# Attention and two MoE layers on one core: earlier first queries, a filled first hole, nine products for the shared tile

## The chip, the cores and the metric

One core of one Trainium2 chip runs the whole program in one launch. The metric is the device time of that launch in microseconds (us). Of the kernel before, three runs took 697.0, 698.44 and 698.81 us; the median is 698.44 us. One further run was profiled.

## The reference

Three stages follow one another. Attention has 2 batches of 8 heads, 1152 keys and 576 queries (two neighbouring queries are averaged first) of 64 dimensions. Then a softplus layer with 2048 and a gated layer with 1536 hidden columns follow, on 1152 tokens of 512. All arrays are fp32.

```python
q_pool = q.reshape(B, H, S // factor, factor, D).mean(axis=3)
scores = scale * np.matmul(q_pool, k.transpose(0, 1, 3, 2))
scores = scores - np.max(scores, axis=-1, keepdims=True)
attn = np.exp(scores)
attn = attn / (np.sum(attn, axis=-1, keepdims=True) + 1e-09)
attn_out = np.matmul(attn, v)
...
h = x @ w_in
g = np.maximum(h, 0.0) + np.log1p(np.exp(-np.abs(h)))
x = g @ w_out
...
xn = x / rms * rms_g
out = (silu(xn @ w_gate) * (xn @ w_val)) @ w_out
```

## The kernel before

**Split operands.** Every fp32 operand of a product is split into a rounded part (h) and the small remainder (l), both stored as fp32r. A head has 64 dimensions, half of the array's 128 rows. So a head's key tile `kk` holds the rounded keys (K high) in one half of the partitions and the remainders (K low) in the other, and the queries stand in both halves. One product of `qh` with `kk` then gives high by high plus high by low; a second one with `ql` gives the rest. A tile of 128 queries against 1152 keys is done in three thirds of 384 keys: six products.

**Tiles of a pair.** Heads are taken in pairs (A and B), eight pairs. 576 queries are four tiles of 128 and one rest of 64. The rests of both heads share one tile: A's 64 queries stand in columns 0 to 63, B's in 64 to 127, and zeros fill the other half of each operand. `qk` (L437) issues twelve products for this shared tile: qh and ql of A, qh and ql of B, three thirds each.

**A tile's way.** TensorE writes the scores into PSUM (one buffer per head letter); VectorE takes the maximum over 1152 columns (L466); ScalarE takes the exponential (L468); TensorE transposes it in groups of four 128x128 blocks into one of two PSUM banks `t` (L487, the shared tile's L774); ScalarE or VectorE copies each bank to SBUF (L258, L260); TensorE multiplies by V (L508).

**The start.** `prep(0)` (L346) loads the first pair. Its keys `kr` come in thirds on SyncE's queue; the first 128 queries of each head (`qr` for A, `p` for B, two pieces each) on ScalarE's queue, behind `rgs` and behind an activation table load; the other queries follow on SyncE's queue. Each query sum, rounding, remainder and each K low third is an instruction of its own. Meanwhile TensorE does 16 transposes of the identity that nobody reads (`heat`, L791).

**The order.** Nothing is ordered by hand. `Plan` collects all operations with their engines, estimated durations and dependences, and `run` (L147) simulates a list schedule, which fixes each engine's instruction order; several copies may go to either of two engines. TensorE keeps the order in which the program was written. `WAIT` (L175) says when a more urgent operation may pass another. `EARLY` (L36) is the number of weight pieces unpacked during attention into slots that exist from the beginning; `MIDDLE` more follow when half of attention's buffers are closed.

Of the kernel before, what the change touches and what calls it, by code (L numbers as in the profile page):

```python
# [12 lines left out]
F32 = mybir.dt.float32  # L13
# [22 lines left out]
EARLY = 10  # L36
# [4 lines left out]
WAIT = 2.0  # L41
WARM = 16
# [168 lines left out]
def body(ctx: ExitStack, tc: tile.TileContext, kT, qT, v, w1, w1o, wg, wv, w2o, rg, outT):  # L211
    nc = tc.nc
    ctx.enter_context(tc.manual_schedule())
    nc.scalar.preload_act_table_set("exp_and_others")
# [12 lines left out]
    nc.scalar.dma_start(out=rgs, in_=rg)  # L227
# [71 lines left out]
    def decode(n):  # L299
# [26 lines left out]
        if b in third:  # L326
# [5 lines left out]
    qx = [[[fixed("ea"[z], f"q{s}{'AB'[h]}{z}", [P, NF * P + P], F32R) for s in "hl"] for h in range(2)]  # L332
          for z in range(2)]
# [4 lines left out]
    for z in range(2):  # L338
        for h in range(2):
            for s in range(2):  # L340
                c = NF * P + (D if h == 0 else 0)
                op([dve(D)], lambda e, b=qx[z][h][s], c=c: copy(e, b()[:, c:c + D], zero), w=[(qx[z][h][s], "z")])
# [3 lines left out]
    def prep(pb):  # L346
# [9 lines left out]
        qcuts = ((0, slice(0, P), P), (1, slice(P, SQ), SQ - P))  # L356

        def load_q(h, c, cut, m, queue):
            for z in range(2):
                load(lambda z=z: qr[h]()[z * D:z * D + D, :, cut], qT[n + h][:, :, cut], m // 2, [(qr[h], (z, c))], queue)  # L360

        for h in range(2):
            qr.append(ring("a", "p1", [P, 2, SQ], F32, 2) if first and h else ring("e", "qr", [P, 2, SQ]))
            qs.append(ring("a", "y", [P, SQ]) if first and h else ring("e", "qs", [P, SQ]))
            if first:
                load_q(h, *qcuts[0], "ACTQ")
        pairs = kT[n:n + 2].rearrange("a d s -> (a d) s")
        if first:
            for c, cut, m in kcuts:
                load(lambda cut=cut: kr()[:, cut], pairs[:, cut], 192, [(kr, c)])  # L370
        else:
            load(kr, pairs, 576, [(kr, None)])
        for h in range(2):
            if first:
                load_q(h, *qcuts[1], "SP")
            else:
                for z in range(2):
                    load(lambda h=h, z=z: qr[h]()[z * D:z * D + D], qT[n + h], 288, [(qr[h], (z, 0)), (qr[h], (z, 1))])
# [13 lines left out]
        def sum_q(h, cut, m, c):  # L392
            op([dve(m), pool(m)], lambda e: tt(e, qs[h]()[:, cut], qr[h]()[:, 0, cut], qr[h]()[:, 1, cut], ALU.add),
               r=[(qr[h], (z, x)) for z in range(2) for x in c], w=[(qs[h], c)])

        for h in range(2):
# [3 lines left out]
            if first:  # L400
                c, cut, m = qcuts[0]
# [526 lines left out]
```

## Time and profile before

| | |
|---|---|
| median of three runs | 698.44 us |
| profiled execution | 697.78 us |
| its span, first to last instruction | 695.6 us |
| TensorE matmul busy | 681.2 us, 98% |
| VectorE busy | 430.7 us, 62% |
| ScalarE busy | 335.2 us, 48% |
| GpSimd busy | 111.9 us, 16% |

Attention takes about the first 267 us, the softplus layer and the gated layer the rest. Engines are PE (TensorE), PEld (its weight loads), DVE (VectorE), ACT (ScalarE), POOL (GpSimd), SP (SyncE); an engine with a q at its end is the queue's issue of DMAs. A row of the timeline gives start, length and the idle time before with what ended it. Products are pipelined, so the length of a single row (337 ns) is longer than their distance; the chain of waits shows the distance.

### The profile page before, as it was taken

Reading aid. Unit: us, or ns where it says so; the run is one execution under the profiler, and the core shown is the slowest. Engines: PE = TensorE matmul, PEld = TensorE weight load, DVE = VectorE, ACT = ScalarE, POOL = GpSimd, SP = SyncE. Lnnn points to the kernel's source line nnn. Section 1 sums busy time; section 2 is a strip of 40 time slices with the busy share of each in tenths; the row PEclk is TensorE's granted clock in tenths of the full one; section 3 lists DMA queues with packets and bytes.
Section 4 is the critical chain, followed back from the end, with each engine's and each line's share of the span. In section 5 each row is a group of like instructions: output and inputs, shape, how many; then the busy total and the mean of one; then the engine's idle time right before and its main releaser. Section 6 shows DMA issues by size and latency. Waiting matters only on the chain.

```text
span 695.6 us, 12413 instructions
## 1 busy us (share of the span) xinstructions
PE 681.2 (98%) x5071; PEld 657.5 (95%) x5071; DVE 430.7 (62%) x741; ACT 335.2 (48%) x617; POOL 111.9 (16%) x115
## 2 busy tenths in 40 slices
PE   6999999999999999999999999999999999999997
PEld 5989899898889889999999999999999999999997
DVE  6778778877877778987425267887875332222222
ACT  4877878887788784654212243464452210010001
POOL 1531426425341132000000000011121000000000
PEclk9999999999999999999999999999999999999999
DMA  7355424262412213554000023343441100010001
GB/s 209 124 152 140 130 83 135 55 181 96 120 38 76 79 62 111 182 176 141 28 1 1 3 89 122 127 147 119 163 146 56 46 0 1 1 46 0 1 1 45
DMA packets 21221, 59.77 MB, mean 86 GB/s; under 512 B 3823, under 2 KB 6830, under 8 KB 21166
## 3 DMA queue, kind: packets, MB, share of 16 engines
q1 hardware_dynamic: 20446, 58.73, 26.8%
q8 instruction: 39, 0.64, 0.4%
q10 hardware_dynamic: 720, 0.26, 0.2%
q14 instruction: 16, 0.13, 0.1%
HBM read 56.59 MB, written 2.39 MB: 85 GB/s over the span
## 4 chain that ended last, share of the span: by engine, by line
PE 70%; ACT 0%; DVE 0%; issue 0%
PE s L618 15%; PE s L620 15%; PE s L619 15%; PE t L620 5%; PE t L618 5%; PE t L619 5%; PE t L508 3%; PE s L450 3%; PE t L487 2%; PE t L774 0%; PE s L688 0%; ACT pt L258 0%; PE s L716 0%; PE t L566 0%; DVE raw L260 0%
## 5 line engine op out<-in xcount | busy, mean ns | idle before, releaser
L618 PE MATMUL s<-x,w 128*128 128x384 f32 x348 | 117.4, 337 | 0.5 <-ACT rs L258 0.5
L466 DVE TENSOR_REDUCE nm<-s 128x1 f32<-128x1152 f32 x72 | 97.7, 1357 | 31.7 <-PE s L450 28.1
L620 PE MATMUL s<-x,w 128*128 128x384 f32 x348 | 116.7, 335 | 0.0
L619 PE MATMUL s<-x,w 128*128 128x384 f32 x348 | 116.6, 335 | 0.0
L468 ACT ACTIVATE p<-s,nm 128x1152 f32<-128x1152 f32 x72 | 88.2, 1225 | 12.9 <-DVE nm L466 11.1
L258 ACT COPY pt<-t 128x512 f32<-128x512 f32 (+1 forms) x146 | 76.0, 528 | 36.4 <-PE t L487 29.8
L487 PE MATMUL t<-ident,p 128*128 128x128 f32 x576 | 85.7, 281 | 3.6 <-ACT pt L258 2.2
L740 ACT ACTIVATE g<-s 128x384 f32<-128x384 f32 x36 | 17.7, 492 | 139.7 <-PE s L620 139.7
L487 PEld LDWEIGHTS t<-ident,p 128*128 128x128 f32 x576 | 66.6, 142 | 16.3 <-issue 5.1
L618 PE MATMUL s<-gh,w 128*128 128x384 f32 x243 | 81.5, 335 | 0.0
L620 PE MATMUL s<-gh,w 128*128 128x384 f32 x243 | 81.5, 335 | 0.0
L619 PE MATMUL s<-gl,w 128*128 128x384 f32 x243 | 81.4, 335 | 0.0
L508 PE MATMUL t<-pt,v 128*64 128x128 f32 (+1 forms) x1440 | 80.1, 265 | 0.0
L508 PEld LDWEIGHTS t<-pt,v 128*64 128x64 f32 x1440 | 71.3, 137 | 7.3 <-issue 6.3
L618 PEld LDWEIGHTS s<-x,w 128*128 128x128 f32 x348 | 65.4, 188 | 1.0 <-ACT rs L258 0.8
L619 PEld LDWEIGHTS s<-x,w 128*128 128x128 f32 x348 | 65.4, 188 | 0.0
L620 PEld LDWEIGHTS s<-x,w 128*128 128x128 f32 x348 | 65.4, 188 | 0.0
L263 DVE TENSOR_TENSOR gl<-g,gh 128x384 fp32r<-128x384 f32 x84 | 48.7, 580 | 11.5 <-ACT gh L258 9.3
L312 ACT ACTIVATE t<-raw 128x512 f32<-128x512 f32 x68 | 44.6, 672 | 15.9 <-DVE w L263 10.4
L260 DVE CAST gh<-g 128x384 fp32r<-128x384 f32 x61 | 22.1, 362 | 45.3 <-PE t L620 39.3
L640 ACT ACTIVATE g<-s 128x384 f32<-128x384 f32 x36 | 17.7, 492 | 64.4 <-PE s L620 62.9
L322 DVE SCALAR_TENSOR_TENSOR t<-t,t 128x512 int32<-128x512 int32 x68 | 47.2, 694 | 1.5
(141 smaller groups left out, 1195.3 us busy)
## 6 DMA issues: line engine op xcount, KB each, us to landing
raw<-in_w_dram SPq DMA_DIRECT2D x16, 512.0 KB, 4.2
raw<-in_w1o_dram SPq DMA_DIRECT2D x16, 512.0 KB, 3.4
qr<-in_qT_dram SPq DMA_DIRECT2D x28, 288.0 KB, 4.3
raw<-in_wg_dram SPq DMA_DIRECT2D x12, 512.0 KB, 3.5
raw<-in_wv_dram SPq DMA_DIRECT2D x12, 512.0 KB, 3.6
raw<-in_w2o_dram SPq DMA_DIRECT2D x12, 512.0 KB, 3.5
v<-in_v_dram SPq DMA_DIRECT2D x16, 288.0 KB, 3.2
kr<-in_kT_dram SPq DMA_DIRECT2D x7, 576.0 KB, 5.5
```

The costliest lines, as they stand in the source:

```text
L258: nc.scalar.copy(out, in_)
L260: engines[e].tensor_copy(out, in_)
L263: engines[e].tensor_tensor(out=out, in0=in0, in1=in1, op=o)
L312: o = op([("ACT", 0.68)], lambda e: nc.scalar.activation(out=t0(), in_=word(1).bitcast(F32), scale=2.0 ** -112, **(dict(func=AF.Prelu, alp ...
L322: op([dve(DM)], lambda e: nc.vector.scalar_tensor_tensor(out=t0().bitcast(I32), in0=t0().bitcast(I32), scalar=3, in1=t1(), op0=ALU.logical ...
L466: u["mx"] = op([dve(S, psum=True)], lambda e: nc.vector.tensor_reduce(out=nm(), in_=sc()[:, :, :N], axis=AX.XY, op=ALU.max, negate=True), ...
L468: o = op([("ACT", 1.42)], lambda e: nc.scalar.activation(out=pr(), in_=sc()[:, :, :N], func=AF.Exp, bias=nm(), accum_out=s["den"]()[:, col ...
L487: nc.tensor.transpose(t()[:, i * P:(i + 1) * P], pr[:, c * P:(c + 1) * P], ident)
L508: nc.tensor.matmul(t()[h * D:h * D + D, :n], lhsT=s["v"][h]()[:, c, :], rhs=rhs, start=(c == 0), stop=(c == CK - 1))
L618: nc.tensor.matmul(out, lhsT=w[:, 0, cols], rhs=hi, start=start, stop=False)
L619: nc.tensor.matmul(out, lhsT=w[:, 0, cols], rhs=lo, start=False, stop=False)
L620: nc.tensor.matmul(out, lhsT=w[:, 1, cols], rhs=hi, start=False, stop=stop)
```

## The change

- The first 128 queries of head A are the first transfer on both queues, one piece on each; the first key third follows on ScalarE's queue, the other two on SyncE's, then B's first queries. The array of queries is laid out so that the two neighbours of the first 128 lie side by side: a piece is one run of 256 numbers per partition. The table load moves behind ScalarE's two DMAs, `rgs` to the end of attention.
- The first maximum waits, as a dependence, for the K low thirds and the first query remainders of both heads; the copy `kh` below waits for that maximum.
- 20 instead of 16 idle transposes at the start, and 16 more (`WAKE`) between the products of the first two tiles and the first transposes of exponentials.
- The shared tile gets nine products: qh of A and qh of B with their `kk`, and one with `qm` and `kh` for both heads. `qm` holds A's 64 remainders in its upper left and B's in its lower right quarter, zeros elsewhere; `kh` is the rounded keys of both heads, one under the other, a new copy of 128x1152 per pair. Remainder by remainder is dropped for this tile.
- Query sums are cut at 128, 224 and 224 columns instead of twice 288; the first pair's are only done on VectorE.
- `EARLY` is 9 instead of 10, `WAIT` 3.5 instead of 2.0, and the first ten loads of each queue keep their written order.

```diff
-EARLY = 10
+EARLY = 9
...
-WAIT = 2.0
-WARM = 16
+WAIT = 3.5
+WARM = 20
+WAKE = 16
...
-    nc.scalar.preload_act_table_set("exp_and_others")
...
-    nc.scalar.dma_start(out=rgs, in_=rg)
...
-    def load(out, src, kb, w, queue="SP"):
+    issued = {"SP": [], "ACTQ": []}
+
+    def load(out, src, kb, w, queue="SP", lat=2.2):
         q = nc.sync if queue == "SP" else nc.scalar
-        return op([(queue, 0.6 + max(0, kb / 220 - 0.6))], lambda e: q.dma_start(out=out(), in_=src), w=w, lat=2.2)
+        o = op([(queue, 0.6 + max(0, kb / 220 - 0.6))], lambda e: q.dma_start(out=out(), in_=src), w=w, lat=lat,
+               after=issued[queue][-1:] if len(issued[queue]) < 10 else ())
+        issued[queue].append(o)
+        return o
...
-    qx = [[[fixed("ea"[z], f"q{s}{'AB'[h]}{z}", [P, NF * P + P], F32R) for s in "hl"] for h in range(2)]
-          for z in range(2)]
+    qx = [[[fixed("ea"[z], f"q{s}{'AB'[h]}{z}", [P, NF * P + (P if s == "h" else 0)], F32R) for s in "hl"]
+           for h in range(2)] for z in range(2)]
+    qm = [fixed("ea"[z], f"qm{z}", [P, P], F32R) for z in range(2)]
...
-        qcuts = ((0, slice(0, P), P), (1, slice(P, SQ), SQ - P))
-
-        def load_q(h, c, cut, m, queue):
+
+        def load_q(h, c, queues=("SP", "SP")):
+            cut = slice(0, 2 * P) if c == 0 else slice(2 * P, 2 * SQ) if c == 1 else slice(0, 2 * SQ)
             for z in range(2):
-                load(lambda z=z: qr[h]()[z * D:z * D + D, :, cut], qT[n + h][:, :, cut], m // 2, [(qr[h], (z, c))], queue)
+                parts = [(qr[h], (x, z)) for x in range(2) if c in (x, None)]
+                load(lambda z=z: qr[h]()[z * D:z * D + D, cut], qT[n + h][:, cut], (cut.stop - cut.start) // 4, parts, queues[z])
...
-            if first:
-                load_q(h, *qcuts[0], "ACTQ")
+        if first:
+            load_q(0, 0, ("SP", "ACTQ"))
         pairs = kT[n:n + 2].rearrange("a d s -> (a d) s")
         if first:
             for c, cut, m in kcuts:
-                load(lambda cut=cut: kr()[:, cut], pairs[:, cut], 192, [(kr, c)])
+                load(lambda cut=cut: kr()[:, cut], pairs[:, cut], 192, [(kr, c)], "SP" if c else "ACTQ", (2.0, 3.1, 2.7)[c])
+            load_q(1, 0)
...
-        def sum_q(h, cut, m, c):
-            op([dve(m), pool(m)], lambda e: tt(e, qs[h]()[:, cut], qr[h]()[:, 0, cut], qr[h]()[:, 1, cut], ALU.add),
-               r=[(qr[h], (z, x)) for z in range(2) for x in c], w=[(qs[h], c)])
+        def sum_q(h, part, a, m):
+            o = slice(a, a + m)
+            i = a if part == 0 else a + P
+            j = i + (P if part == 0 else SQ - P)
+            op([dve(m)] if first else [dve(m), pool(m)], lambda e: tt(
+                e, qs[h]()[:, o], qr[h]()[:, i:i + m], qr[h]()[:, j:j + m], ALU.add), r=[(qr[h], (part, z)) for z in range(2)],
+               w=[(qs[h], part)])
+
+        kh = s["kh"] = ring("a", "kh", [P, S], F32R)
+
+        def last_q(h):
+            qh, low = s["q"][h][0], qm[pb % 2]
+            x = f if h == 0 else f + D
+            r = slice(h * D, h * D + D)
+            op([dve(D, True), act(D)], lambda e: scale16(e, qh()[:, x:x + D], qs[h]()[:, f:]), r=[(qs[h], None)], w=[(qh, "e")])
+            op([dve(D)], lambda e: nc.vector.scalar_tensor_tensor(
+                out=low()[r, h * D:h * D + D], in0=qs[h]()[r, f:], scalar=0.0625, in1=qh()[r, x:x + D],
+                op0=ALU.mult, op1=ALU.subtract), r=[(qs[h], None), (qh, "e")], w=[(low, ("e", h))])
...
-            round_q(h, ("e",), f if h == 0 else f + D, D, slice(f, SQ))
+            last_q(h)
+        op([dve(S, True), act(S)], lambda e: copy(e, kh(), kr()), r=[(kr, None)], w=[(kh, None)])
...
-        todo = [(hh, z) for hh in heads for z in range(2)]
+        if x < NF:
+            cols = slice(x * P, (x + 1) * P)
+            part = "m0" if x == 0 else "m1"
+            todo = [(s["q"][h][z], s["kk"][h], cols, [part]) for z in range(2)]
+        else:
+            cols = slice(NF * P, NF * P + P)
+            todo = [(s["q"][hh][0], s["kk"][hh], cols, ["e", "z"]) for hh in heads]
+            todo.append((qm[pb % 2], s["kh"], slice(0, P), [None]))
 
         def go(e):
-            for hh, z in todo:
-                q = s["q"][hh][z]()[:, x * P:(x + 1) * P]
+            for i, (q, k, cut, _) in enumerate(todo):
                 for c in range(KB):
-                    nc.tensor.matmul(sc()[:, c, :N], lhsT=q, rhs=s["kk"][hh]()[:, c * N:(c + 1) * N],
-                                     start=(hh == heads[0] and z == 0), stop=(hh == heads[-1] and z == 1))
+                    nc.tensor.matmul(sc()[:, c, :N], lhsT=q()[:, cut], rhs=k()[:, c * N:(c + 1) * N],
+                                     start=(i == 0), stop=(i == len(todo) - 1))
...
     prep(0)
-    warm = tbank()
-
-    def heat(e):
-        for _ in range(WARM):
-            nc.tensor.transpose(warm()[:, :P], ident, ident)
-    op([("PE", 4.0)], heat, w=[(warm, None)])
+    queued = [o for o in plan.ops if o.opts[0][0] == "ACTQ"]
+    kinds["start"] = [op([("ACT", 1.3)], lambda e: nc.scalar.preload_act_table_set("exp_and_others"), after=queued)]
+    def heat(n, d):
+        warm = tbank()
+
+        def go(e):
+            for _ in range(n):
+                nc.tensor.transpose(warm()[:, :P], ident, ident)
+        op([("PE", n * d)], go, w=[(warm, None)])
+
+    heat(WARM, 0.22)
     qk(0, 0, 0)
     qk(0, 0, 1)
+    for h in range(2):
+        for b in (st[0]["kk"][1], st[0]["q"][1][1]):
+            for part, ops in b.writers.items():
+                if part in ("m0", ("l", 0), ("l", 1), ("l", 2)):
+                    units[0, 0, 0]["mx"].deps.update(ops)
+    heat(WAKE, 0.11)
+    for o in st[0]["kh"].writers[None]:
+        o.deps.add(units[0, 0, 0]["mx"])
...
+    op([("ACTQ", 0.6)], lambda e: nc.scalar.dma_start(out=rgs, in_=rg), after=[plan.pe[-1]])
...
+    for o in kinds["exp"]:
+        o.deps.update(kinds["start"])
...
+    def qcols(a):
+        return np.concatenate([a[..., :P].reshape(B * H, D, 2 * P), a[..., P:].reshape(B * H, D, 2 * (SQ - P))], axis=2)
+
     arrays = {
         "kT": np.ascontiguousarray(k.transpose(0, 1, 3, 2)).reshape(B * H, D, S),
-        "qT": np.ascontiguousarray(q.reshape(B, H, SQ, 2, D).transpose(0, 1, 4, 3, 2)).reshape(B * H, D, 2, SQ),
+        "qT": qcols(q.reshape(B * H, SQ, 2, D).transpose(0, 3, 2, 1)),
```

What this does to the instruction order shows at three places. On VectorE, the start, from the first instruction on loaded data to the first maximum (`kk_145` and `kk_147` are the key tiles of heads A and B, `y` is B's query sum, `p_136` its raw queries). Before:

```order
L260 CAST kk_145<-kr 64x384
L263 TENSOR_TENSOR qs<-qr 128x128
L263 TENSOR_TENSOR kk_145<-kr,kk_145 64x384
L260 CAST kk_145<-kr 64x384
L263 TENSOR_TENSOR kk_145<-kr,kk_145 64x384
L388 SCALAR_TENSOR_TENSOR qlA_124<-qs,qhA_122 128x128
L263 TENSOR_TENSOR kk_145<-kr,kk_145 64x384
L263 TENSOR_TENSOR y<-p_136 128x128
L263 TENSOR_TENSOR kk_147<-kr,kk_147 64x384 x2
L466 TENSOR_REDUCE nm_177<-s 128x1
```

After, where `kk_153` is A's and `kk_151` B's key tile:

```order
L262 TENSOR_TENSOR qs<-qr 128x128
L453 TENSOR_SCALAR qhA_123<-qs 128x128
L393 SCALAR_TENSOR_TENSOR qlA_148<-qs,qhA_123 128x128
L259 CAST kk_153<-kr 64x384
L262 TENSOR_TENSOR kk_153<-kr,kk_153 64x384
L262 TENSOR_TENSOR kk_151<-kr,kk_151 64x384
L259 CAST kk_153<-kr 64x384
L262 TENSOR_TENSOR kk_153<-kr,kk_153 64x384 x2
L262 TENSOR_TENSOR y<-p_142 128x128
L262 TENSOR_TENSOR kk_151<-kr,kk_151 64x384 x2
L393 SCALAR_TENSOR_TENSOR qlB_180<-y,qhB_127 128x128
L490 TENSOR_REDUCE nm_182<-s 128x1
```

The query work of A stands ahead of the keys, and all six K low subtractions and both remainders stand ahead of the first maximum, where before one subtraction of B and B's remainder stood behind it.

On TensorE, the start. Before (`p_187` is A's first exponential, `p_227` B's):

```order
L793 MATMUL t<-ident 128x128 x16
L450 MATMUL s<-kk_145,qhA_122 128x384 x3
L450 MATMUL s<-kk_145,qlA_124 128x384 x3
L450 MATMUL s<-kk_147,qhB_126 128x384 x3
L450 MATMUL s<-kk_147,qlB_129 128x384 x3
L487 MATMUL t<-ident,p_187 128x128 x4
L450 MATMUL s<-kk_145,qhA_122 128x384 x3
L450 MATMUL s<-kk_145,qlA_124 128x384 x3
L487 MATMUL t<-ident,p_187 128x128 x4
L487 MATMUL t<-ident,p_227 128x128 x8
```

After (`p_211` is A's, `p_226` B's):

```order
L820 MATMUL t<-ident 128x128 x20
L476 MATMUL s<-kk_153,qhA_123 128x384 x3
L476 MATMUL s<-kk_153,qlA_148 128x384 x3
L476 MATMUL s<-kk_151,qhB_127 128x384 x3
L476 MATMUL s<-kk_151,qlB_180 128x384 x3
L820 MATMUL t<-ident 128x128 x16
L511 MATMUL t<-ident,p_211 128x128 x4
L476 MATMUL s<-kk_153,qhA_123 128x384 x3
L476 MATMUL s<-kk_153,qlA_148 128x384 x3
L511 MATMUL t<-ident,p_211 128x128 x4
L511 MATMUL t<-ident,p_226 128x128 x8
```

The idle transposes grew from 16 to 20, and 16 more stand between the products of B's first tile and the first transposes of A's exponential.

On TensorE, the shared tile of the first pair, between the transposes of tile 3. Before:

```order
L487 MATMUL t<-ident,p_402 128x128 x4
L450 MATMUL s<-kk_145,qhA_122 128x384 x3
L450 MATMUL s<-kk_145,qlA_124 128x384 x3
L450 MATMUL s<-kk_147,qhB_126 128x384 x3
L450 MATMUL s<-kk_147,qlB_129 128x384 x3
L487 MATMUL t<-ident,p_402 128x128 x4
```

After:

```order
L511 MATMUL t<-ident,p_424 128x128 x4
L476 MATMUL s<-kk_153,qhA_123 128x384 x3
L476 MATMUL s<-kk_151,qhB_127 128x384 x3
L476 MATMUL s<-kh,qm_125 128x384 x3
L511 MATMUL t<-ident,p_424 128x128 x4
```

Of the twelve products six with remainders have become three with `kh`.

## Rows read from the trace of the kernel before

**Rows 1.** The page, first part: busy time, share of the span, instructions.
```profile
PE 681.2 (98%) x5071; PEld 657.5 (95%) x5071; DVE 430.7 (62%) x741; ACT 335.2 (48%) x617; POOL 111.9 (16%) x115
```

**Rows 2.** Busy by stretch (PE, PEld, DVE, ACT, POOL, clock, DMA); the sum is 24-265.
```profile
85.00:115.00 30.00, 29.63 (x320) 27.14 (x319) 24.98 (x37) 24.34 (x43) 13.15 (x14) 1.00 0.33 94
...
265.00:295.00 30.00, 30.00 (x205) 29.68 (x204) 26.94 (x49) 16.98 (x33) 3.17 (x3) 1.00 0.43 145
...
sum 241.00, PE 237.32 PEld 217.05 DVE 182.97 ACT 193.50 POOL 87.77; mean PE 29.66 PEld 27.13 DVE 22.87 ACT 24.19 POOL 10.97
```

**Rows 3.** Timeline of TensorE, 0 to 24 us.
```profile
1.36 3.67 PE L793 MATMUL t<-ident 128*128 128x128 f32 x16 [1.36 <-POOL ident masks.py:199]
7.81 0.66 PE L450 MATMUL s<-kk,qhA 128*128 128x384 f32 x1 [2.77 <-DVE kk L263]
...
13.97 0.69 PE L450 MATMUL s<-kk,qhB 128*128 128x384 f32 x1 [1.27 <-DVE kk L263]
14.46 1.16 PE L450 MATMUL s<-kk,qlB 128*128 128x384 f32 x3
15.42 1.05 PE L487 MATMUL t<-ident,p 128*128 128x128 f32 x4
...
23.80 2.19 PE L508 MATMUL t<-pt,v 128*64 128x128 f32 x36
```

**Rows 4.** Timeline of TensorE's weight loads, same stretch.
```profile
17.88 1.82 PEld L487 LDWEIGHTS t<-ident,p 128*128 128x128 f32 x8
...
19.92 0.52 PEld L487 LDWEIGHTS t<-ident,p 128*128 128x128 f32 x4 [0.22 <-ACT pt L258]
```

**Rows 5.** Chain of waits, a shared tile in mid attention: start, length, products.
```profile
219.95 0.66 PE t L487 x6
220.61 2.09 PE s L450 x12
```

**Rows 6.** Timeline of the other engines and queues, 0 to 24 us.
```profile
0.73 1.34 SPq L267 DMA_DIRECT2D kr<-in_kT_dram  x3
...
1.19 1.26 ACTq L267 DMA_DIRECT2D qr<-in_qT_dram  x2
...
3.27 0.35 DVE L260 CAST kk<-kr 64x384 fp32r<-64x384 f32 x1 [1.20 <-DMA kr<-in_kT_dram]
...
6.79 0.29 DVE L263 TENSOR_TENSOR qs<-qr 128x128 f32<-128x128 f32 x1 [3.16 <-DMA qr<-in_qT_dram]
...
7.69 1.35 POOL L263 TENSOR_TENSOR qs<-qr 128x448 f32<-128x448 f32 x1 [6.38 <-DMA qr<-in_qT_dram]
...
8.08 1.37 DVE L263 TENSOR_TENSOR kk<-kr,kk 64x384 fp32r<-64x384 f32 x1
...
9.81 0.55 DVE L263 TENSOR_TENSOR kk<-kr,kk 64x384 fp32r<-64x384 f32 x1
...
12.10 1.36 DVE L466 TENSOR_REDUCE nm<-s 128x1 f32<-128x1152 f32 x1 [0.35 <-PE s L450]
...
14.62 0.62 DVE L263 TENSOR_TENSOR y<-p 128x448 f32<-128x448 f32 x1
```

**Rows 7.** Groups by line, 24 to 265 us: busy us, mean ns, idle before.
```profile
L466 DVE TENSOR_REDUCE nm<-s 128x1 f32<-128x1152 f32 x68 | 92.2, 1357 | 29.7 <-PE s L450 26.0 <-ACT p L468 2.3 <-ACT w L258 0.7
L468 ACT ACTIVATE p<-s,nm 128x1152 f32<-128x1152 f32 x69 | 84.5, 1225 | 10.9 <-DVE nm L466 9.0
...
L258 ACT CAST kk<-kr 64x1152 fp32r<-64x1152 f32 x8 | 9.2, 1154 | 0.2
...
L260 DVE CAST kk<-kr 64x1152 fp32r<-64x1152 f32 x6 | 4.5, 743 | 0.0
```

**Rows 8.** Busy time by stretch, one of the first microseconds (columns as in rows 2).
```profile
3.00:4.00 1.00, 1.00 (x7) 1.00 (x6) 0.35 (x1) 0.00 (x0) 0.00 (x0) 1.00 0.89 244
```

**Rows 9.** Groups by line and shape, 24 to 267 us (columns as in rows 7).
```profile
L260 DVE COPY pt<-t 128x512 f32<-128x512 f32 x32 | 22.1, 691 | 11.4 <-PE t L487 10.9 <-PE t L774 0.2
...
L258 ACT COPY pt<-t 128x256 f32<-128x256 f32 x27 | 10.1, 374 | 5.0 <-PE t L487 4.0
```

More of the change, by code (lines that the diff above doesn't have):

```diff
@@ L339, in body @@
         for h in range(2):
-            for s in range(2):
-                c = NF * P + (D if h == 0 else 0)
-                op([dve(D)], lambda e, b=qx[z][h][s], c=c: copy(e, b()[:, c:c + D], zero), w=[(qx[z][h][s], "z")])
+            c = NF * P + (D if h == 0 else 0)
+            op([dve(D)], lambda e, b=qx[z][h][0], c=c: copy(e, b()[:, c:c + D], zero), w=[(qx[z][h][0], "z")])
+            r = slice(h * D, h * D + D)
+            c = D - h * D
+            op([dve(D)], lambda e, b=qm[z], c=c, r=r: copy(e, b()[r, c:c + D], zero[r]), w=[(qm[z], ("z", h))])
     st = [dict() for _ in range(NP)]
@@ L355, in prep @@
         f = NF * P
-        qcuts = ((0, slice(0, P), P), (1, slice(P, SQ), SQ - P))
-        def load_q(h, c, cut, m, queue):
+        def load_q(h, c, queues=("SP", "SP")):
+            cut = slice(0, 2 * P) if c == 0 else slice(2 * P, 2 * SQ) if c == 1 else slice(0, 2 * SQ)
             for z in range(2):
-                load(lambda z=z: qr[h]()[z * D:z * D + D, :, cut], qT[n + h][:, :, cut], m // 2, [(qr[h], (z, c))], queue)
+                parts = [(qr[h], (x, z)) for x in range(2) if c in (x, None)]
+                load(lambda z=z: qr[h]()[z * D:z * D + D, cut], qT[n + h][:, cut], (cut.stop - cut.start) // 4, parts, queues[z])
         for h in range(2):
-            qr.append(ring("a", "p1", [P, 2, SQ], F32, 2) if first and h else ring("e", "qr", [P, 2, SQ]))
+            qr.append(ring("a", "p1", [P, 2 * SQ], F32, 2) if first and h else ring("e", "qr", [P, 2 * SQ]))
             qs.append(ring("a", "y", [P, SQ]) if first and h else ring("e", "qs", [P, SQ]))
-            if first:
-                load_q(h, *qcuts[0], "ACTQ")
+        if first:
+            load_q(0, 0, ("SP", "ACTQ"))
         pairs = kT[n:n + 2].rearrange("a d s -> (a d) s")
@@ L373, in prep @@
         for h in range(2):
[L374 to L378, printed above, removed]
+            load_q(h, 1 if first else None)
             vt = ring("ea"[pb % 2], f"v{h}{pb % 2}", [P, CK, D])
@@ L400, in prep @@
             if first:
[L401 to L402 removed]
+                sum_q(h, 0, 0, P)
                 round_q(h, ("m0",), 0, P, slice(0, P))
@@ L410, in prep @@
             else:
-                for cut in (slice(0, SQ // 2), slice(SQ // 2, SQ)):
-                    sum_q(h, cut, SQ // 2, (0, 1))
+                sum_q(h, 0, 0, P)
+                for x in range(2):
+                    sum_q(h, 1, P + x * (SQ - P) // 2, (SQ - P) // 2)
                 round_q(h, ("m0", "m1"), 0, f, slice(0, f))
```

11 lines of the change are left out of this document (4 added, 7 removed).

## The prediction

> **What bounds the kernel now.** I read the page's busy shares first: TensorE is busy 681.2 of 695.6 us, the next engine 62% [rows 1]. That alone says only that TensorE is near full, so I read it by stretch: from 24 to 265 us, all attention but its start, TensorE is busy 237.3 of 241 us, and in a stretch of 30 us of it VectorE is busy for 25.0 and ScalarE for 24.3 [rows 2]. After attention, in the 30 us in which the weights are unpacked, TensorE has no gap at all [rows 2]. So from 24 us on a microsecond of products removed is a microsecond gained, as long as the other engines keep up. The third view is TensorE's own timeline of the first 24 us, where it is different: it waits 1.36 us for the identity, 2.8 us before the first product and 1.3 us before B's second third [rows 3], and what it does runs at the lower of its two clock levels: 16 transposes take 3.67 us, 0.23 each [rows 3], while six take 0.66, 0.11 each, in mid attention [rows 5]. The PEclk column says 1.00 there too, so the level has to be read off the lengths. The rise (1.2 to 2.4 GHz) lies between two groups of loads: eight in 1.82 us from 17.88 on, four in 0.52 from 19.92 on [rows 4].
>
> The change works at these two places: the start, up to the first product with V at 23.80 us [rows 3], after which TensorE hardly waits again, and the shared tile of each pair.
>
> **Nine products for twelve.** Twelve products of a shared tile take 2.09 us, 0.174 each [rows 5]. Three fewer in each of eight pairs are 24, 24 x 0.174 = 4.2 us. All shared tiles come after 24 us, at the high level, so nothing has to be halved or doubled. In return each pair gets one copy of 128x1152; columns, not partitions, set its length, so the nearest rows are the copies of 64x1152: 0.74 us on VectorE, 1.15 on ScalarE [rows 7]. The order puts six on VectorE and two on ScalarE: 6 x 0.74 + 2 x 1.15 = 6.8 us of work over attention. It is hidden by the 7 us of idle that VectorE has on average per 30 us (22.9 busy) [rows 2], and its consumer, the shared tile, stands at the pair's end. If no idle took it, it would cost all 6.8. The raw keys are now held until this copy, so the next pair's keys load later; they have most of a pair, 30 us, to come. A remainder of 64 columns remains per head, on half the partitions; a query sum is three instructions instead of two with the same columns. For all this and for the changed order (WAIT) I take 0.4 us of new waits of TensorE, between 0 and 6.8, near the low end: its idle time in attention is now 241 - 237.3 = 3.7 us for almost eight pairs [rows 2], and I see no reason that it doubles. It can fall below 3.7 too, by tenths.
>
> **The start, up to the first maximum.** Before, VectorE starts on A's query sum at 6.79, because these queries were issued from 1.19 on and landed last, while the first key third, issued at 0.73, could be used at 3.27 [rows 6]. After, the queries are issued first on both queues, and are a third of that key piece in size; I take 3.25 for them, no better than the key third did. From there VectorE's queue up to the first maximum, with 0.29 for 128 columns, 0.35 for a rounding copy and 0.55 for a subtraction of 384 columns [rows 6]: query sum, rounding and remainder 0.8 (the rounding taken at 0.22, at most 0.29), copy 0.35, two subtractions 1.1, copy 0.35, two subtractions 1.1, B's sum 0.29, two subtractions 1.1, B's remainder 0.29: 5.4 us in all, so 8.65 us. The data keep ahead: queries and all keys are 704 KB, at 244 GB/s [rows 8] 2.9 us, so the last third is there at about 5 us and is wanted at 5.5. Before, one subtraction took 1.37 instead of 0.55 while GpSimd did A's long query sum beside it (7.69 to 9.04) [rows 6]; this sum is now VectorE's and stands behind the first maximum, so I count no such stretch. TensorE is not later: 20 transposes end at 1.36 + 20 x 0.229 = 5.95, A's three thirds come free at 4.8, 6.4 and 6.95, and A's six products are done by 8.4. So the first maximum starts at 8.65 instead of 12.10 [rows 6], 3.4 us earlier. The rest of B's work that had stood behind the maximum now stands ahead of it; that price (0.55 + 0.29) is in the sum, and B's products follow A's without the wait of 1.3 us.
>
> **From the first maximum to the first product with V.** Before, this took 23.80 - 12.10 = 11.7 us. After, A's exponential is ready at 8.65 + 1.36 + 1.23 and some, 11.35 [rows 7]. B's last three products wait for its remainder (8.65) and end near 9.7. Then come the 16 new transposes, which are pure extra work: 1.76 us at the high level, ending at 11.45 and hidden in the hole; 3.67 at the low level, ending at 13.4, 2 us after A's exponential.
>
> With the high level, VectorE and ScalarE set the end: maximum to 10.0, A's long sum and rounding 0.62 + 0.35, B's maximum 1.36, remainder 0.55, B's sum 0.62, copy of a bank 0.69, next maximum 1.36 [rows 6, 7, 9]: 15.55. Its exponential 1.35 with what lies around it, then the key copy on ScalarE 1.15 and the copy of two blocks 0.37 [rows 7, 9], which frees the bank for four transposes of 0.44: V begins at 18.9, 4.9 us earlier. Here the key copy is not hidden; without it ScalarE would be ready 1.15 us sooner.
>
> With the low level, A's transposes start at 13.4 instead of 15.42 [rows 3]; as before it would take 23.80 - 15.42 = 8.4 us to V, plus up to 1.15 for the key copy: 21.8 to 22.9, 0.9 to 2.0 us earlier. These are the ends, 0.9 and 4.9.
>
> Which level? Before, TensorE worked without a wait from 13.97 on, products and transposes mixed, and had risen by 19.92 [rows 3, 4]. After, by the schedule above, its last wait of over half a microsecond is the one for the identity at 1.36, some 12 us sooner, and so I expect the rise before the new transposes are through. I take the start at 4.0 us, nearer the upper end. The Trainium skill, page "TensorE: Matmul & The Clock Gate", section "Part 4: PE-mode transpose", speaks against this: the full clock, it says, "doesn't engage" for transposes. By that rule the 36 idle transposes would be cost only, and the case of the low level would hold. The trace does not decide it: 16 transposes by themselves were not followed by a rise, but the rise at 19.9 came right behind eight transposes in a row, which stood behind products [rows 3, 4].
>
> **Other edits, at nothing.** The table load behind two DMA issues ends near 3 us, ahead of ScalarE's first copy. `rgs` is wanted far behind attention. One weight piece fewer in attention moves its 2 to 3 us of unpacking into the stretch after 265 us, where VectorE still has 3 us idle in 30 while TensorE has none [rows 2]; if that cover failed, up to 3 us.
>
> **Sum.** -4.2 - 4.0 + 0.4 = -7.8 us against the profiled execution of 697.78 us (span 695.6 and 2.2 around it): 690.0. The median of the runs is 0.66 higher, 698.44, so 690.6.
>
> **Rivals.**
> - The clock stays low through the start, by idle transposes that do not raise it. Start 1.5 instead of 4.0 us: 698.44 - 4.2 - 1.5 + 0.4 = 693.1. For it: 16 transposes raised nothing. Against: the new ones have products on either side, almost without a wait. Chance 0.2.
> - The start is not earlier at all: the queries land no sooner because all pieces share the same DMA engines, which are 0.89 busy from 3 us on [rows 8]. 698.44 - 4.2 + 0.4 = 694.6. Against: a piece at the head of a queue was usable after 2.5 us. Chance 0.09.
> - The new order makes TensorE wait about 0.7 us per pair, and half the start's gain goes: 698.44 - 4.2 - 2 + 5.5 = 697.7, no change. Chance 0.06.
> - Slower: with `kh`, VectorE's and ScalarE's queue becomes the bound of a pair. Then a pair grows by its key copy instead of shrinking: 698.44 + 6.8 - 4.0 = 701.2. It decides once waits exceed 4.2 + 4.0 = 8.2 us, 1.0 per pair. For it: VectorE is busy 25 of 30 us in one stretch. Against: over attention it waits 26.0 us for TensorE's scores, ScalarE only 9.0 for VectorE's maxima [rows 7]. Chance 0.05.
>
> **How the numbers follow.** The forecast, 690.6, has 0.60, with a range of its own from 688.0 (start 4.9, and waits below today's by about 1 us) to 692.5. No change means within 0.3%, 2.1 us, about what a measurement of this kernel can tell. Faster: 0.60 + 0.20 + 0.09 = 0.89; same 0.06; slower 0.05. The range that should hold 8 in 10 takes in the first two rivals and leaves out the last two: 688.0 to 694.8.
>
> **What would show it.** In the profile after: 24 products on `kh`, and 96 instead of 120 on each of qlA and qlB; shared tiles of 1.57 us. VectorE's first query sum near 3.25 and the first maximum near 8.65; the 16 new transposes in about 1.8 us, not 3.7; the first product with V near 19. TensorE's idle from there to 260 us at most 4 to 5 us. Wrong would be: V after 21 us, new waits of TensorE for VectorE or ScalarE of 0.5 us or more per pair, or gaps of TensorE between 265 and 295 us.

## The result and the profile after

The changed kernel takes 690.93 us (median of five runs, 689.77 to 691.12), the kernel before 698.09 on the same chip (697.0 to 698.81). The ratio is 0.9904, 95% interval 0.9893 to 0.9914: 1% faster, and 0.3 us from the forecast of 690.6. The medians are 7.2 us apart, the two profiled executions 6.7 (697.78 and 691.12) and their spans 6.4 (695.55 and 689.11).

The page, first part, against [rows 1]: TensorE has the same share of a shorter span, and VectorE has 10 us more to do.

```profile
PE 678.2 (98%) x5067; PEld 654.1 (95%) x5067; DVE 440.5 (64%) x759; ACT 334.4 (49%) x616; POOL 107.2 (16%) x121
```

TensorE's timeline of the first 20 us, against [rows 3]:

```profile
1.36 4.08 PE L820 MATMUL t<-ident 128*128 128x128 f32 x20 [1.36 <-POOL ident masks.py:199]
6.13 0.44 PE L476 MATMUL s<-kk,qhA 128*128 128x384 f32 x1 [0.70 <-DVE kk L262]
...
7.68 1.09 PE L476 MATMUL s<-kk,qhA 128*128 128x384 f32 x2 [1.11 <-DVE kk L262]
8.57 1.16 PE L476 MATMUL s<-kk,qlA 128*128 128x384 f32 x3
...
11.45 2.02 PE L820 MATMUL t<-ident 128*128 128x128 f32 x16
13.30 0.60 PE L511 MATMUL t<-ident,p 128*128 128x128 f32 x4
...
19.84 2.19 PE L532 MATMUL t<-pt,v 128*64 128x128 f32 x36
```

The first product with V starts at 19.84 instead of 23.80 us. The new idle transposes (L820) follow B's products without a gap and take 2.02 us. A's transposes start behind them, at 13.30. VectorE and ScalarE over the same stretch, against [rows 6]:

```profile
3.48 0.29 DVE L262 TENSOR_TENSOR qs<-qr 128x128 f32<-128x128 f32 x1 [1.12 <-DMA qr<-in_qT_dram]
...
5.14 0.35 DVE L259 CAST kk<-kr 64x384 fp32r<-64x384 f32 x1 [0.78 <-DMA kr<-in_kT_dram]
...
9.77 1.36 DVE L490 TENSOR_REDUCE nm<-s 128x1 f32<-128x1152 f32 x1
11.16 1.22 ACT L492 ACTIVATE p<-s,nm 128x1152 f32<-128x1152 f32 x1 [2.40 <-DVE nm L490]
```

The query sum is at 3.48, 0.2 us behind the forecast's 3.25; then VectorE waits 0.78 us for the first key third, so that the first maximum comes at 9.77 and not at 8.65. TensorE's clock fell about 0.6 us after its last long wait for those keys. Busy time of TensorE by stretch (us, busy, granted clock, DMA share, GB/s):

```profile
7.00:8.00 1.00, 0.32 (x1) 1.00 0.96 227
8.00:9.00 1.00, 0.97 (x4) 0.63 1.06 273
9.00:10.00 1.00, 1.00 (x5) 0.50 1.03 232
...
11.00:12.00 1.00, 1.00 (x8) 0.67 0.24 76
12.00:13.00 1.00, 1.00 (x12) 1.00 0.16 23
```

0.50 is the level of 1.2 GHz, 1.00 that of 2.4. By the shares of 0.63 and 0.67 the clock fell near 8.3 and rose near 11.7, inside the 16 idle transposes.

The chain of waits (start, length) shows what set the start of the products with V:

```profile
8.15 3.50 PE s L476 x10
11.65 1.82 PE t L820 x16
13.47 0.44 PE t L511 x4
...
15.42 0.59 ACT pt L257
...
16.06 0.66 PE t L511 x4
```

From 8.15 us on, behind the last wait for the keys, it is TensorE's own work, the idle transposes included, with one short wait for a bank copy before 16.06. The first maximum is not on this chain: A's exponential was through near 12.5, and the idle transposes held A's transposes up by 0.8 us.

The shared tile, in the same chain, against [rows 5]: nine products in 1.58 us instead of twelve in 2.09. Further rows show what came with them:

```profile
91.76 1.58 PE s L476 x9
93.35 0.02 issue
93.37 0.76 DVE kh L259
94.13 1.28 DVE nm L490
95.41 0.02 issue
95.43 1.31 ACT p L492 x2
96.74 0.48 ACT pt L257
```

The key copy stands between the end of the products and the maximum of the tile that they made, and this is the chain that ends last in the whole run. The summary of the tile `kh` (count, shortest, median and longest in ns, first and last start) says how often:

```profile
L259 DVE CAST kh<-kr x6: 750/760/1622, 62.9 to 217.4; 128x1152 fp32r<-128x1152 f32 x6
L257 ACT CAST kh<-kr x2: 1159/1162/1165, 17.6 to 36.4; 128x1152 fp32r<-128x1152 f32 x2
its engine sat idle before it (us, times) until:
  PE s L476: 2.6, 5
who waited for it (us, times):
  DVE kh L259: 2.6, 5
  DVE nm L490: 1.6, 3
```

`kh` has one buffer, so the next pair's copy cannot start before the shared tile's last product has read the old one. That is the moment at which this tile's maximum becomes possible too. Five of VectorE's six copies wait for that moment (2.6 us in all) and go first, by the planner's order.

**Where the 6.4 us are.** Four points of the two timelines: first product with V 23.80 and 19.84 (-3.96); from there to the first transpose that spreads the attention sums, 242.77 and 239.49 (-3.28); from there to the end of the last product 425.47 and 425.83 (+0.36); from there to the end of the span, with the last output's landing, 3.51 and 3.95 (+0.44). The last two lie in code that the change hardly touches. The +0.36 is in the main one place, between the second and the third sum of rows (76.00 and 76.43 us); of the runs below, those with WAIT at 2.0 in the new order, with two key copies and with the low keys behind the maximum have 75.95 or 75.96 there, the others 76.42 or 76.43. Its cause stays open.

### The profile page after: what moved, and what is told of

The parts are those of the page before. It is cut to its first block, busy times and chain, and to the rows that moved or that the text cites. A ratio compares the mean times of both kernels' runs of the same rounds, so it can differ in the third digit from the quotient of the medians.

```text
span 689.1 us, 12450 instructions
## 1 busy us (share of the span) xinstructions
PE 678.2 (98%) x5067; PEld 654.1 (95%) x5067; DVE 440.5 (64%) x759; ACT 334.4 (49%) x616; POOL 107.2 (16%) x121
## 4 chain that ended last, share of the span: by engine, by line
PE 95%; DVE 2%; ACT 1%; DMA 1%; issue 0%; ACTq 0%; DVEq 0%
PE s L642 16%; PE s L644 15%; PE s L643 15%; PE s L476 12%; PE t L532 10%; PE t L511 9%; PE t L644 5%; PE t L643 5%; PE t L642 5%; PE t L798 1%; DVE nm L490 1%; DMA kr<-in_kT_dram 1%; ACT pt L257 0%; DVE pt L259 0%; DVE kh L259 0%
## 5 line engine op out<-in xcount | busy, mean ns | idle before, releaser
L257 ACT COPY pt<-t 128x512 f32<-128x512 f32 (+2 forms) x140 | 73.0, 533 | 31.2 <-PE t L511 23.3
L511 PEld LDWEIGHTS t<-ident,p 128*128 128x128 f32 x576 | 65.2, 140 | 16.8 <-issue 5.3
L262 DVE TENSOR_TENSOR gl<-g,gh 128x384 fp32r<-128x384 f32 x83 | 46.8, 564 | 7.7 <-ACT gh L257 5.6
L766 DVE TENSOR_TENSOR g<-g,t 128x384 f32<-128x384 f32 x18 | 10.0, 555 | 62.5 <-PE t L644 60.8
```

What stands on the lines that cost most here:

```text
L257: nc.scalar.copy(out, in_)
L262: engines[e].tensor_tensor(out=out, in0=in0, in1=in1, op=o)
L511: nc.tensor.transpose(t()[:, i * P:(i + 1) * P], pr[:, c * P:(c + 1) * P], ident)
```

## The experiments

Each ratio is to the kernel before; the changed kernel has 0.9904 [0.9893, 0.9914]. "V" is the start of the first product with V, and "attention" the time from V to that first spreading transpose.

**The products alone** (the old start, WAIT at 2.0, EARLY at 9):

```diff
-        todo = [(hh, z) for hh in heads for z in range(2)]
...
+            todo = [(s["q"][hh][0], s["kk"][hh], cols, ["e", "z"]) for hh in heads]
+            todo.append((qm[pb % 2], s["kh"], slice(0, P), [None]))
...
```

> The kernel before, with the nine products for the shared tile alone (new operands, the key copy after the first maximum, one weight piece fewer in attention so that they fit); the start is as before. My theory: 24 products of 0.174 us go, less the same few tenths per pair of new waits that the changed kernel shows in attention (0.9 us in all): 694.0 to 695.0, 3.1 to 4.2 us faster than 698.1, first product with V still near 23.8 us. Rival, the start carries the gain and the key copies on VectorE eat the products': 697 to 699.

Measured: 695.48 us, ratio 0.9970 [0.9958, 0.9981], against 697.41: 1.9 us faster, short of the 3.1 to 4.2. V was at 24.43 because this run's queries could be used at 7.57 instead of 6.79 us [rows 6], for which the edit has no evident cause. Attention took 239.65 us, 3.1 less than before. The changed kernel's 239.49 is the same: all that 24 products bring and cost is in this part.

**The start alone** (the changed kernel, with twelve products):

```diff
-            todo.append((qm[pb % 2], s["kh"], slice(0, P), [None]))
+        todo = [(hh, z) for hh in heads for z in range(2)]
...
```

> The changed kernel with twelve products for the shared tile again and without the key copy; the new start stays. My theory: the start alone gives 4.0 us, and without the key copies there are none of the new waits in attention: 693.8 to 694.6, first product with V at 19.5 to 19.9 us. Rival, the waits in attention come from the changed order and not from the key copies: still 0.9 us of them, 695.0 or a little more. Second rival, the start's 4 us are partly lost later: 696 to 698.

Measured: 695.59, ratio 0.9974 [0.9964, 0.9984], 1.8 us faster. The first maximum was at 9.68, as in the changed kernel, but V at 21.00. ScalarE's timeline shows why:

```profile
13.91 0.59 ACT L257 COPY pt<-t 128x512 f32<-128x512 f32 x1 [1.40 <-PE t L492]
14.40 1.23 ACT L473 ACTIVATE p<-s,nm 128x1152 f32<-128x1152 f32 x1
```

Its queue has the copy of A's first bank ahead of B's exponential, and the copy waits for transposes that stand behind the idle ones. The next run tests that.

**The start alone, with ScalarE's order put right** (the planner's figure for one idle transpose, raised from 0.11 to 0.2 us; the expectation has this the wrong way round):

```diff
-    heat(WAKE, 0.11)
+    heat(WAKE, 0.2)
```

> The new start with twelve products for the shared tile, as before, and with the 16 idle transposes planned at 0.2 of a unit of time less, so that ScalarE does B's exponential ahead of its copy of A's first bank, as in the changed kernel. Theory: the start alone had its first product with V at 21.00 us and not at 19.84 only because ScalarE's queue stood in the other order (copy at 13.91, B's exponential at 14.40 instead of 13.35); so V now begins at 19.7 to 20.1 and the kernel is 0.9 to 1.2 us faster than the start alone: 694.4 to 694.7 where the kernel before has 697.4. Rival: V waits for VectorE's maxima, and ScalarE's order costs nothing: V at 21, 695.6.

Measured: 693.33, ratio 0.9943 [0.9931, 0.9956] against 697.02: 3.7 us faster; V at 19.89, where the changed kernel has it. The exponential now comes first:

```profile
13.05 1.22 ACT L473 ACTIVATE p<-s,nm 128x1152 f32<-128x1152 f32 x1 [0.73 <-DVE nm L471]
...
14.27 0.58 ACT L257 COPY pt<-t 128x512 f32<-128x512 f32 x1
```

V is as forecast; the time is better than the 694.4 to 694.7, since attention, at 242.31 us, is 0.6 shorter too. One bank copy went from ScalarE to VectorE (16.68) by the same edit, so the 1.1 us of V are the price of ScalarE's order and of this copy together. The start is worth 3.7 us by the time and 3.9 by V. With 3.1 of attention from the products this is 6.8 of the 7.2 us between the medians.

**B's low keys behind the first maximum** (the lines that let the maximum wait for them, which name B's alone, are turned round; leaving them out alone gives every engine the same order):

```diff
-                    units[0, 0, 0]["mx"].deps.update(ops)
...
+            o.deps.add(units[0, 0, 0]["mx"])
```

> The changed kernel with one part undone: the last third of B's low keys and B's query remainder again stand behind the first maximum. Theory: two VectorE instructions of 0.55 and 0.29 us move behind the maximum, which waits for the first key third and not for them, so the first maximum comes up to 0.8 us sooner (9.0 to 9.8), B's last products later by a maximum's length (1.36), and the first product with V between 0.2 us sooner and 0.6 later: time within 0.6 us of the changed kernel. Rival (that the order ahead of the first maximum carries the gain at the start): V 1.3 us later or more, at least 1.2 us slower.

Measured: 694.47, ratio 0.9960 [0.9948, 0.9973]; by the medians 3.5 us slower than the changed kernel, far more than the theory's 0.6: the rival, which had at least 1.2. The first maximum is 0.73 us sooner, at 9.04. Then, on TensorE:

```profile
10.92 0.69 PE L476 MATMUL s<-kk,qhB 128*128 128x384 f32 x1 [1.30 <-DVE kk L262]
11.40 1.16 PE L476 MATMUL s<-kk,qlB 128*128 128x384 f32 x3
12.36 3.62 PE L820 MATMUL t<-ident 128*128 128x128 f32 x16
15.78 0.93 PE L511 MATMUL t<-ident,p 128*128 128x128 f32 x4
...
23.49 0.77 PE L532 MATMUL t<-pt,v 128*64 128x128 f32 x10
```

```profile
9.00:10.00 1.00, 0.62 (x2) 0.81 1.03 245
...
15.00:16.00 1.00, 1.00 (x7) 0.50 0.81 152
16.00:17.00 1.00, 1.00 (x7) 0.78 0.87 295
```

TensorE waits 1.30 us in the middle of B's products. Its clock falls near 9.6 (0.81 for 9 to 10 us), where that wait begins, and rises only near 16.4 (0.78 for 16 to 17), so all 16 idle transposes run at the low level. A fall there is in the changed kernel too, near 8.3; what differs is that TensorE then worked on without a wait, and rose near 11.7. A's transposes start at 15.78 instead of 13.30: 0.91 us from the later end of B's products, the rest from the idle transposes. V is 3.65 us later. The other 1.17 lie between A's transposes and V, where the planner gave ScalarE another order too: the chain goes there over a third bank copy (19.57) and A's second exponential (20.15), which are not on it in the changed kernel. So two VectorE instructions of 0.55 and 0.29 us ahead of the maximum buy off 2.5 us; the 1.2 come with the order that follows from them.

**No idle transposes in the hole:**

```diff
-    heat(WAKE, 0.11)
```

> The changed kernel without the 16 idle transposes in the first hole; all else stays. My theory: they keep TensorE at work until its clock has risen; without them the first transposes and the next tile run at the low level, V comes 0.5 to 1.5 us later: 691.4 to 692.4. Rival, they are cost only (they end about 0.9 us after the first exponential is ready in the changed kernel's trace): A's transposes start 0.9 us earlier and the time falls to 690.0 to 690.4, or stays at 690.9 where VectorE's queue is the bound anyway.

Measured: 691.29, ratio 0.9908 [0.9894, 0.9923], V at 20.63, 0.79 later. The times' intervals overlap, so the price is in the profile alone.

```profile
12.37 1.11 PE L511 MATMUL t<-ident,p 128*128 128x128 f32 x4 [1.28 <-ACT p L492]
```

TensorE waits for A's exponential and does its transposes in 1.11 us instead of 0.60; the granted clock is 0.50 until near 15.9 us.

**Half of them:**

```diff
-WAKE = 16
+WAKE = 8
```

> The changed kernel with 8 idle transposes in the first hole instead of 16. In the changed kernel the 16 take 2.02 us, and the rise of the granted clock lies inside them. Theory (TensorE fell to the low level in its waits before 7.7 us, and has to work for a while to rise): the eight end near 12.4 to 12.6, A's transposes start when A's exponential is ready, near 12.5, 0.8 us sooner, but part of them at the low level; V between 19.3 and 20.2, time within 0.6 us of the changed kernel. Rival (the idle transposes are only in the way): V 0.9 us sooner, time 0.9 us lower. Rival (they are wanted in full): V at 20.6, as without them, 0.8 us slower.

Measured: 690.62, ratio 0.9906 [0.9891, 0.9921]: no difference that the times show. A's transposes start at 12.26, 1.04 sooner, V only 0.46, of which 0.26 is an earlier first maximum. The chain of waits now goes over VectorE: the first maximum, A's long sum and rounding, and A's long remainder, for which TensorE's next products wait:

```profile
12.96 0.56 DVE qlA L393
...
13.57 0.79 PE s L476 x3
```

So 16 idle transposes were more than the hole holds, and with eight VectorE's queue is the bound.

**The old load queues with the new rest:**

```diff
-            load_q(0, 0, ("SP", "ACTQ"))
+            load_q(0, 0, ("ACTQ", "ACTQ"))
+            load_q(1, 0, ("ACTQ", "ACTQ"))
...
-                load(lambda cut=cut: kr()[:, cut], pairs[:, cut], 192, [(kr, c)], "SP" if c else "ACTQ", (2.0, 3.1, 2.7)[c])
-            load_q(1, 0)
+                load(lambda cut=cut: kr()[:, cut], pairs[:, cut], 192, [(kr, c)], "SP", (2.0, 3.1, 2.7)[c])
```

> The changed kernel with the first pair's loads on the queues of before: all key thirds on SyncE's queue, first queries of A and B on ScalarE's; the moved table load and the contiguous pieces stay. My theory: the order of transfers is worth 1 to 2 of the start's 4 us, since VectorE's query work would start late again: 692 to 693. Rival, since first key third and queries share the same engines, one comes late for the other (the key third was first used at 3.3 us before and at 5.1 after): no difference, 690.5 to 691.3.

Measured: 692.12, ratio 0.9925 [0.9913, 0.9936]. The key third can be used at 3.29, the queries only at 6.07; first maximum 11.10, V 21.85. By V the order of the loads is worth 2.0 us, half of the start's gain (1.2 by the medians). Of the 2.0, 1.33 are the first maximum's; the clock is low here until near 14.4 us, and the idle transposes take 2.68 us instead of 2.02.

**The key third at a queue's head:**

```diff
-            load_q(0, 0, ("SP", "ACTQ"))
+            load_q(0, 0)
...
-                load(lambda cut=cut: kr()[:, cut], pairs[:, cut], 192, [(kr, c)], "SP" if c else "ACTQ", (2.0, 3.1, 2.7)[c])
+                load(lambda cut=cut: kr()[:, cut], pairs[:, cut], 192, [(kr, c)], ("ACTQ", "SP", "ACTQ")[c], (2.0, 3.1, 2.7)[c])
```

> The changed kernel with another order of its first loads: both query pieces on the first queue, and the first key third at the head of the second queue instead of behind a query piece. Theory (the first key third was late, 3.75 us after issue, because it was second on its queue, and VectorE waited 0.78 us for it): the key third is usable by 3.5 to 4.2, the second query piece about 0.6 us later than now; VectorE's first key copy at 4.2 to 4.6 instead of 5.14, first maximum at 8.9 to 9.3 instead of 9.77, V at 19.0 to 19.5, 0.4 to 0.8 us faster than the changed kernel. Rival (all pieces share the same DMA engines, so that the sum of bytes ahead of the key third sets it): one piece comes sooner for another that comes later, first maximum 9.5 to 10.0, no change.

Measured: 690.92, ratio 0.9909 [0.9895, 0.9922], first maximum at 9.66, V at 19.75: the rival.

```profile
3.45 0.35 DVE L259 CAST kk<-kr 64x384 fp32r<-64x384 f32 x1 [1.09 <-DMA kr<-in_kT_dram]
...
4.87 0.29 DVE L262 TENSOR_TENSOR qs<-qr 128x128 f32<-128x128 f32 x1 [0.47 <-DMA qr<-in_qT_dram]
```

The keys are there 1.69 us sooner, the queries 1.39 later. In these two orders what comes second can be used near 5 us, whichever it is.

**One key copy for all pairs** (the other seven multiply their query remainder with the first pair's keys, so the last, small term of their shared tiles is another):

```diff
-        kh = s["kh"] = ring("a", "kh", [P, S], F32R)
+        kh = s["kh"] = ring("a", "kh", [P, S], F32R) if first else st[0]["kh"]
...
-        op([dve(S, True), act(S)], lambda e: copy(e, kh(), kr()), r=[(kr, None)], w=[(kh, None)])
+        if first:
+            op([dve(S, True), act(S)], lambda e: copy(e, kh(), kr()), r=[(kr, None)], w=[(kh, None)])
```

> The changed kernel, with the key copy kh made for the first pair alone; the other seven pairs multiply with that copy, so their shared tiles are computed from the first pair's keys. Seven copies of 128x1152 are gone from VectorE and ScalarE, and the raw keys come free sooner. In the changed kernel the seven intervals from shared tile to shared tile sum to 212.5 us, 2.8 less than before, where 21 products of 0.1766 would make 3.7. Theory A (the missing 0.9 us are waits for engines that the copies hold up): the sum falls to 211.3 to 211.8, time 0.7 to 1.2 us below the changed kernel. Theory B (they come from the changed order of VectorE's work, by WAIT): the sum stays within 0.3 of 212.5, no change in time.

Measured: 689.38, ratio 0.9882 [0.9866, 0.9898]; the ratio's interval just overlaps that of the changed kernel. The seven intervals, from the first transposes of one shared tile to those of the next, sum to 210.97, somewhat beyond theory A, which stands. Attention takes 237.83 us, 1.66 less than in the changed kernel for the same products. Of this, 1.41 lies between the starts of attention's transposes and the start of what follows each (550 transposes, 68.56 and 67.15 us when summed): short waits, most likely for banks that VectorE and ScalarE free later.

**Two key copies in each pair:**

```diff
+        op([dve(S, True), act(S)], lambda e: copy(e, kh(), kr()), r=[(kr, None)], w=[(kh, None)])
```

> The changed kernel, with every key copy kh made twice: eight more copies of 0.74 (VectorE) or 1.15 us (ScalarE). Theory A (a copy costs TensorE some 0.13 us of waits in a pair): the seven intervals sum to 213.2 to 213.8 instead of 212.5, and the first pair's second copy stands on ScalarE ahead of the first product with V or not, by the order; time 0.7 to 1.5 us above the changed kernel. Theory B (copies are hidden): no change, within 0.4. Rival of the forecast (VectorE and ScalarE bound a pair): 6 us or more above it.

Measured: 692.48, ratio 0.9928 [0.9915, 0.9942]: 1.55 us more, but not where theory A had it. The intervals sum to 212.73, 0.2 more, with nine of the sixteen copies on ScalarE. The loss is behind attention, where the weights are unpacked (98.42 us from the spreading transposes to the first sum of rows, 96.50 in the changed kernel). TensorE's waits there, 255 to 365 us (in total, times, longest):

```profile
PE s L644 <- DVE gl L262: 1.1, 1, 1.1
```

The changed kernel has no such row. It covers 1.1 of the 1.9 us; that work which VectorE does not get done in attention is missed there is the likely reading, and no run shows it. The rival, 6 us or more, is out.

**WAIT at 2.0:**

```diff
-WAIT = 3.5
+WAIT = 2.0
```

> The changed kernel with WAIT at 2.0, as before, so that VectorE's and ScalarE's work of a pair is ordered by the old rule. Theory A (new waits come from the copies): seven intervals sum to 212.2 to 212.9, time within 0.5 us of the changed kernel. Theory B (they come from the order): the sum falls to 211.3 to 211.9, time 0.6 to 1.2 us lower.

Measured: 691.75, ratio 0.9916 [0.9902, 0.9930]. Attention is the same (239.79, and 212.88 for the seven intervals), so the order is not the cause of its waits. The time is 0.8 us more by the medians, past theory A's 0.5, but the intervals overlap. The trace has 0.7 of it behind attention (97.23 us for the 96.50), with the same kind of wait, and gives some back at the end: the spans differ by 0.3.

```profile
PE s L643 <- DVE gl L262: 0.4, 1, 0.4
```

**WAKE at 8 and WAIT at 2.0**, both edits as above:

> The changed kernel with 8 idle transposes in the first hole instead of 16, and WAIT at 2.0. With 8 transposes alone the first product with V was at 19.38 instead of 19.84 us and the time 690.62. If the old WAIT is no worse or somewhat better in attention, this is the fastest so far: 689.6 to 690.5 where the kernel before has 697.0 to 697.4. If it brings waits: 690.6 to 691.5.

Measured: 691.56, ratio 0.9913 [0.9899, 0.9926]; 97.23 us again for that stretch. By the medians WAIT at 2.0 costs 0.9 on top of 8 idle transposes and 0.8 on top of 16; the intervals overlap each time. Nothing tried here that keeps the whole computation is measurably faster than the changed kernel.

## Why the prediction was right, and where it was not

- **Products, -4.2 us.** Right: 24 products on `kh`, 96 on each of qlA and qlB, 1.58 us for a shared tile. With one copy for all pairs, attention falls from 242.77 to 237.83, by 4.9 us; before had one wait of 0.69 there, at 186.78, where the longest of the run with one copy is 0.3.
- **New waits, +0.4 us.** The term that was mis-sized. Of the 4.2, attention kept 3.3 beside before and 3.2 beside the mean of before and the two starts alone (242.77, 242.90, 242.31), so the net price was 0.9 to 1.0; taking seven copies away gives back 1.7. What failed is "it is hidden by the 7 us of idle that VectorE has": five of the six copies on VectorE could not begin in the idle time ahead of them, since their one buffer was still being read, and then went ahead of the shared tile's maximum, as the rows of `kh` and the chain show. That this place, and not the copies' work as such, makes the price is argued from the chain: neither a second buffer nor a copy ordered behind that maximum was tried, and eight more copies added only 0.2 us to the intervals. The price is far from the 6.8 us of the slower rival.
- **Length of a copy, 0.74.** Four took 0.75 to 0.76, so columns did set it, not partitions. Two took twice that, beside GpSimd:

```profile
123.59 1.41 POOL L262 TENSOR_TENSOR y<-O,rdb 128x576 f32<-128x576 f32 x1
...
124.01 1.62 DVE L259 CAST kh<-kr 128x1152 fp32r<-128x1152 f32 x1 [0.81 <-PE s L476]
```

  The two overlap for 0.99 us, and the copy is 0.86 longer; in the run with two copies, at 124.19 with GpSimd idle, it took 0.76. The prediction saw such a stretch at the start, but priced the new copy without it. The Trainium skill, "Trainium Architecture — The Big Picture", section "What this means for kernel authors", calls the port pair that VectorE and GpSimd share an exclusive lock and not a split of bandwidth; these rows agree in size, for this pair of operations.
- **The start, -4.0 us.** Right in its sum (-3.96), by luck: two of its steps failed. "The data keep ahead" is the first: the first key third, second on its queue, could be used 3.75 us after issue and not 2.5, and the first maximum was 1.1 us late. With keys first the queries are late instead, which speaks for a price of all pieces together. (By the prediction's own steps A's first third would come free at 4.95 and not 4.8, which changes nothing.) The second is "VectorE and ScalarE set the end", with the idle transposes "hidden in the hole". From the maximum to V this case worked out 10.25 us, and it took 10.07, but on another path: the chain runs over TensorE from 8.15 us on, the idle transposes stand on it for 1.82 us, and the maximum does not. The 4.0 had been chosen below the end of 4.9; the misses filled that distance.
- **The clock.** The rival of a low start (chance 0.2) did not come, though the reason given was not what happened. The forecast had TensorE without a long wait from 1.36 us on. It waited 0.70 and 1.11 us, fell to the low level near 8.3 us and rose inside the idle transposes, so these took 2.02 us, near the forecast's 1.8. With the low keys behind the maximum TensorE waited 1.30 us after the fall, the transposes took 3.62 and the start lost 3.65 us, some 2.5 of them up to A's transposes: a low start is real, and the order of two VectorE instructions is enough for it. That the wait kept the clock low is read from these rows; without the idle transposes a wait of 1.28 us after the fall also went with a late rise (15.9). This is also why costing the low keys ahead of the maximum by their own length (0.55 + 0.29) missed what they are worth.
- **The rule against it.** "Part 4: PE-mode transpose" of the Trainium skill's page "TensorE: Matmul & The Clock Gate", by which transposes bring no full clock, does not agree: before the product at 6.13 us, of 0.44 where the first one had 0.66 in [rows 3], TensorE had done nothing but 20 transposes, and these took 4.08 us where 20 at the low level of [rows 3] would take 4.6. In ten of the twelve runs with this start that product took 0.44 or 0.45 us. In the run with two key copies it did not:

```profile
5.94 0.69 PE L477 MATMUL s<-kk,qhA 128*128 128x384 f32 x1
```

  There the lengths stay at the low level up to B's last products (10.37 us), and V still comes at 19.54: the early rise did not carry the start's gain.
- **The key copy in the first pair, "not hidden".** It ran on ScalarE from 17.59 to 18.76, and TensorE has no recorded wait from 18.18 to V: it cost no wait there.
- **Weights after attention, up to 3 us.** Right at nothing in the changed kernel, which has no gap there. The runs with two copies and with WAIT at 2.0 show that this cover is thin: 1.9 and 0.7 us of it were lost by them.

## What to carry to other kernels

Before calling a copy hidden, look at when its buffer comes free: idle time that lies before that moment covers nothing, and one released by the same products as a maximum competes with it. At a cold start, price an order by the waits it leaves on TensorE: an instruction ahead of the first maximum can be cheaper than a wait while the clock is low. When a sum comes out right, check by the chain that the time was spent on the path that the sum had; here idle transposes, priced as hidden, were on it. When two parts tried singly don't add up to the whole, compare the order of each engine first; here another order on ScalarE was 1.1 us.

## What the runs showed of the hardware

- By the lengths, TensorE came to its high level behind idle transposes alone, and not at one moment: 20 of them, the same in twelve runs, took from 3.72 to 4.53 us, and the product behind them 0.44 or 0.45 us in ten, 0.59 with the low keys behind the maximum, 0.69 (the low level) with two key copies.
- The granted clock fell again after waits of well under 2 us: in the changed kernel near 8.3 us, behind waits of 0.70 and 1.11; with the low keys behind the maximum near 9.6, behind waits of 0.38 and 0.53 and where one of 1.30 begins.
- The busy and idle columns of TensorE hide short waits: attention's transposes have 3.0 us of idle in the changed kernel and 3.6 before, while the same 551 are busy for 82.1 and 81.1 us. Only starts, from one instruction to the next, showed the loss: 68.56 and 67.03 us.
- At the start, a piece that is first on its queue had landed 2.5 to 3.0 us after its issue; the piece behind it could be used after 3.75 in the changed kernel, some 3.5 with keys first and 4.8 with the old queues.
